# A hand-ordered retention and channel-mix kernel on one core: a different word order, block 5 in one chunk, all scaling on VectorE

## The chip, the cores and the metric

The kernel runs on one core of a Trainium2 chip. A core has TensorE (PE, matrix products; its weight loads are shown apart as PEld), VectorE (DVE), ScalarE (ACT), GpSimd (POOL) and SyncE (SP). Each works through its own list of instructions in order and waits on semaphores for the others. The metric is device microseconds (us) of one execution; lower is better.

## The reference

Retention with a decaying state per head, then a token-shifted channel mix:

```python
for t in range(S):                      # B, H, S, D = 4, 8, 768, 64
    state = gamma * state + outer(k[t], v[t])
    y[t] = scale * q[t] @ state
x = y as (B, S, 512)
xk = mu_k * x + (1 - mu_k) * x_prev     # x_prev: x one token earlier
xr = mu_r * x + (1 - mu_r) * x_prev
k = relu(xk @ w_k)                      # 512 -> 1024
v = (k * k) @ w_v                       # 1024 -> 512
out = sigmoid(xr @ w_r) * v             # w_r: 512 -> 512
```

## The kernel before

The 4 x 768 tokens are cut into 12 blocks of 256 tokens, three to a batch entry; the state is carried from block to block inside an entry. The whole program is one list of words, ORDER. A loop at the end of the kernel reads it from left to right and lets each word issue the instructions of one step, so ORDER sets the order on every engine and on the two queues that issue loads and stores (GpSimd and SyncE). No scheduler moves anything; the framework only adds the semaphore waits that data and buffers need.

A word is a code with numbers, then the PSUM banks after @, or the engine after ~ (v VectorE, a ScalarE, p GpSimd, s SyncE). `K.0.3@7` is key group 3 of block 0 into bank 7. The codes, with block n first:

| code | function (line of its instructions) | what it does | engine |
|---|---|---|---|
| lq, lk, lv | load (L232, L237) | q, k, v of a block from DRAM; two DMAs where it is split, one else. EARLY halves go through k2s and are cast by cq, ck | GpSimd or SyncE queue |
| wk, wr, wv | load_wk, load_wr, load_wv | the weights, w_k and w_v in halves | GpSimd queue |
| vs | scale_v (L255) | v times powers of gamma | VectorE or GpSimd |
| Tq, Tk, Eq, Ek | trans, turned_q, turned_k (L274, L280, L243) | transpose q, k and copy out of PSUM | PE, ScalarE |
| S, M | scores (L320, L333, L341), masked (L349, L356) | scores and their mask | PE, VectorE |
| C, U, G | state (L368, L386, L397), summed (L421, L245), decayed (L426) | the chunk's part of the state, its sum, its decay to the next block | PE, VectorE or ScalarE |
| I, Y, J | inter_off, intra, inter_on (L443, L464, L480, L491) | the output from the state and from the scores | PE |
| D, dx | yout (L509, L516), differ (L531) | x from PSUM, its difference to the token before | VectorE |
| X.n.w.j | mixed (L560) | quarter j of the mixed input, w 0 for keys, 1 for the gate | VectorE |
| K, Qa, Qb | keys (L574, L584), relued (L593), squared (L601, L605) | products with w_k, relu, square | PE, ScalarE |
| R, s | gate (L614), opened (L620) | products with w_r, sigmoid | PE, ScalarE |
| V, O, st | values (L626), result (L632), store (L639) | half the products with w_v, times the gate, store of 128 tokens | PE, VectorE, SyncE queue |
| Vc, Oc, sc | values_c (L644), result_c (L651), store_c (L659) | the same for a cut of the last tokens' columns | PE, VectorE, a queue |
| gy, mu, mt, me | powers (L708, L718, L711), load_mu, trans_mu, copy_mu | constants | |
| z.c | zeros (L693, L700) | products with zeros; c // 4 of them in f32, c % 4 in f16, written to a bank and read by nobody | PE |

A block is worked in one of three ways. HALF cuts it into chunks of 64 tokens (one M, up to four U, two D instructions), WIDE into chunks of 128 (two M, two U where a block of its entry follows, one D), and blocks 0 and 1 in a third way, with 128 columns but 64 rows. GROUPS pairs blocks whose X and K are issued once for both. Q16, K16, V32 are rings of four buffers, VS, QT, KT of three, DX of two, XM of three; k2s holds three blocks of squared keys.

Of the kernel before, what the change touches and what calls it, by code (L numbers as in the profile page):

```python
# [53 lines left out]
Qa.6.1 Qb.6.1 K.6.2@6 Qa.6.2 lq.10~p O.3.1 U.8.1 st.1.0 X.5.1.0 X.5.1.2 lk.10~p U.8.2 I.8@01 O.3.0  # L54
st.2.1 Tq.9@23 Eq.9~a O.4.1 Qb.6.3 S.8@45 M.8~v K.6.0@7 K.6.6@6 Qa.6.0 Qb.6.0 Qa.6.6 X.6.1.3
S.9@23 st.3.1 Tq.11@45 Y.8 Eq.11~a X.6.1.2 R.5.1@7 s.5.1 K.6.7@6 Qb.6.2 K.6.4@4 Qa.6.4 M.9~v D.8~v
dx.8~v X.8.0.0 X.8.0.3 X.8.0.1 X.8.1.1 V.5.0.0@5 R.5.0@7 K.6.5@4 s.5.0 X.6.1.1 Tk.10@01 Qa.6.7
lv.10~p vs.10~v X.6.1.0 C.9@23 U.9.0~v Ek.10~a st.3.0 Tq.10@67 V.5.0.1 O.5.0 X.8.0.2 V.5.1.0@0
R.6.1@1 Qa.6.5 U.9.1 U.9.2 U.9.3 Eq.10~a V.5.1.1 st.5.0 O.5.1 s.6.1 Qb.6.4 S.10@45 I.9@67 C.10@23
G.9~a vs.11~v U.10.0 U.10.1 U.10.2 Qb.6.5 M.10~v st.5.1 R.6.0@1 s.6.0 R.7.0@0 s.7.0 K.8.1@1 Qa.8.1  # L60
K.8.2@2 Qa.8.2 C.11@01 I.10@45 U.10.3 Y.9 K.8.0@3 D.9~v Qb.6.7 K.8.3@2 st.4.1 Tk.11@67 G.10~a
U.11.0 U.11.1 Qa.8.0 Ek.11~a U.11.2 Y.10 D.10~v R.7.1@3 s.7.1 dx.9~v dx.10~v X.9.1.1 I.11@01
X.8.1.0 S.11@67 M.11~v X.9.0.0 Qb.8.2 V.7.0.0@4 Qa.8.3 X.9.0.2 X.9.0.1 V.7.1.0@5 V.6.0.0@3 X.9.0.3
Qb.8.1 Qb.6.6 V.6.1.0@2 V.7.1.1 X.8.1.2 V.7.0.1 V.6.0.1 V.6.1.1 K.9.5@6 K.9.7@7 Qb.8.0 st.4.0
# [725 lines left out]
```

## Time and profile before

| | us |
|---|---|
| runs of the kernel before | 155.8, 156.06, 156.61 (median 156.06) |
| profiled execution, own time | 156.68 |
| its span, first to last instruction | 154.9 |
| granted TensorE clock, mean | 1.00 |

| stretch, us | PE busy | VectorE busy | ScalarE busy | GpSimd busy | moved, GB/s |
|---|---|---|---|---|---|
| 5 to 10 | 3.83 of 5 | 3.00 | 3.28 | 4.85 | 250 |
| 20 to 25 | 4.87 of 5 | 4.83 | 4.92 | 3.61 | 213 |
| 70 to 80 | 9.91 of 10 | 9.76 | 7.52 | 6.83 | 142 |
| 100 to 110 | 9.97 of 10 | 9.11 | 7.97 | 0 | 109 |
| 145 to 150 | 5.00 of 5 | 2.25 | 1.68 | 0 | 232 |

A matmul's row shows it from its start to a modelled end, so PE can show as busy while its next operand is awaited; distances from start to start tell more. GpSimd's busy time is the issuing of its DMAs (about 0.9 us each) and two scalings. Loads on the GpSimd queue land in the order of their issue; the median from issue to landing is 7 to 8 us for q, k and v. In the profile's names, ps is PSUM, a the masked scores, tg and t the state, xT the retention output, kr the relued keys, rs the opened gate, os the result.

### The profile page before, as it was taken

The page shows a single profiled execution, that of the slowest core. Times are in us where ns is not written, and L with a number is a line of the kernel's source. Part 1 is how long each engine was busy: PE and PEld are TensorE (multiplying, and loading weights), DVE is VectorE, ACT ScalarE, POOL GpSimd, SP SyncE. Part 2 cuts the span into 40 slices and gives each one's busy share as a digit, 9 for nine tenths or more (in the row PEclk, how much of TensorE's full clock was granted, in tenths as well). Part 3 has the DMA queues.
Part 4 walks back from the last instruction along what each step waited for, and adds up shares of the span by engine and source line. Part 5 has one row for each costly group of instructions (what it writes and reads, how often), then busy time and mean ns, then how long its engine had stood idle before and what let it go on. Part 6 is the DMA issues. An engine that isn't in the chain of part 4 may idle for free.

```text
span 154.9 us, 5520 instructions
## 1 busy us (share of the span) xinstructions
PE 146.0 (94%) x2423; PEld 83.9 (54%) x2423; DVE 126.9 (82%) x205; ACT 99.4 (64%) x186; POOL 55.5 (36%) x65
## 2 busy tenths in 40 slices
...
GB/s 144 263 219 194 197 228 171 196 241 218 156 180 212 199 241 258 223 234 181 116 147 204 150 68 4 4 74 203 4 4 0 6 82 136 52 0 72 96 209 169
DMA packets 45768, 22.31 MB, mean 144 GB/s; under 512 B 37416, under 2 KB 41392, under 8 KB 45744
## 3 DMA queue, kind: packets, MB, share of 16 engines
...
## 4 chain that ended last, share of the span: by engine, by line
PE 55%; DVE 24%; DMA 12%; issue 4%; POOL 3%; DVEq 0%; POOLq 0%
PE ps L626 19%; DMA v<-in_v_dram 12%; PE ps L614 9%; PE ps L574 9%; PE ps L584 8%; DVE a L356 3%; DVE xk L560 3%; DVE xr L560 3%; DVE vs L255 3%; DVE dx L531 2%; DVE xT L516 2%; DVE tg L421 2%; DVE os L632 2%; PE ps L443 2%; DVE a L349 1%
## 5 line engine op out<-in xcount | busy, mean ns | idle before, releaser
L626 PE MATMUL ps<-wv,k2s 128*128 128x512 f16 x184 | 43.4, 379 | 0.0
L593 ACT ACTIVATE kr<-ps 128x512 f32<-128x512 f32 x48 | 27.8, 596 | 23.1 <-PE ps L574 18.0
L626 PEld LDWEIGHTS <-k2s 128*128 128x128 f16 x184 | 17.4, 98 | 20.0
L632 DVE SCALAR_TENSOR_TENSOR os<-ps,rs 128x512 f32<-128x512 f32 x23 | 15.4, 683 | 14.5 <-ACT rs L620 7.4
L614 PE MATMUL ps<-wr,xr 128*128 128x512 f16 x96 | 24.1, 380 | 0.0
L584 PE MATMUL ps<-xk,wk 128*128 128x256 f16 x192 | 24.0, 273 | 0.0
L232 POOL DMA_DIRECT2D k<-in_k_dram x20 | 17.7, 898 | 15.2 <-PE ps L280 10.5
L574 PE MATMUL ps<-xk,wk 128*128 128x512 f16 x96 | 22.5, 379 | 0.0
L584 PEld LDWEIGHTS <-wk 128*128 128x128 f16 x192 | 18.1, 98 | 4.9 <-DMA wk<-in_moe_w_k_dram 0.6
L620 ACT ACTIVATE rs<-ps 128x512 f32<-128x512 f32 x24 | 13.7, 594 | 9.3 <-PE ps L614 8.9
L560 DVE SCALAR_TENSOR_TENSOR xr<-dx,mu,xT 128x256 f16<-128x256 f32 (+1 forms) x36 | 19.2, 564 | 0.1
L560 DVE SCALAR_TENSOR_TENSOR xk<-dx,mu,xT 128x256 f16<-128x256 f32 (+1 forms) x36 | 18.8, 567 | 0.2
L232 POOL DMA_DIRECT2D v<-in_v_dram x18 | 16.2, 915 | 1.4 <-DMA q<-in_q_dram 0.5
L243 ACT COPY kT<-ps 128x1024 f16<-128x1024 f16 (+1 forms) x13 | 12.2, 947 | 5.2 <-PE ps L280 4.1
L601 ACT ACTIVATE k2s<-kr 128x512 f16<-128x512 f32 x24 | 14.9, 628 | 0.3
L574 PEld LDWEIGHTS <-wk 128*128 128x128 f16 x96 | 9.2, 98 | 10.8
L531 DVE TENSOR_TENSOR dx<-xT 128x1024 f32<-128x1024 f32 x12 | 14.6, 1223 | 0.3
L605 ACT ACTIVATE k2s<-kr 128x512 f16<-128x512 f32 x24 | 14.5, 628 | 0.1
L243 ACT COPY qT<-ps 128x1024 f16<-128x1024 f16 (+1 forms) x13 | 12.3, 949 | 2.4 <-PE ps L274 2.2
L614 PEld LDWEIGHTS <-xr 128*128 128x128 f16 x96 | 8.8, 97 | 9.2 <-DVE xr L560 0.2
L255 DVE TENSOR_TENSOR vs<-v,csm_sb 128x1024 f16<-128x1024 f32 x10 | 12.1, 1216 | 2.0 <-DMA v<-in_v_dram 2.0
L356 DVE TENSOR_TENSOR a<-ps,c_sb 128x1024 f16<-128x1024 f32 (+1 forms) x12 | 12.2, 1040 | 0.5 <-PE ps L333 0.4
...
## 6 DMA issues: line engine op xcount, KB each, us to landing
...
wk<-in_moe_w_k_dram POOLq DMA_DIRECT2D x2, 512.0 KB, 11.0
...
```

The source lines that it names most:

```text
L232: e.dma_start(out=dst[:, :, i * D : i * D + D], in_=src[:, i * P : i * P + P].rearrange("h p d -> p h d"),)
L243: e.copy(out=out, in_=in_)
L255: e.tensor_tensor(out=VS(n), in0=V32(n).rearrange("p h (i d) -> p i h d", i=2), in1=gks[:, int(half(n) or wide(n)), :, :, None].to_broadca ...
L356: nc.vector.tensor_tensor(out=a_full(n)[:, i, :, j0:j1], in0=pairs(banks("S", n, i, j0))[:, :, j0:j1], in1=(below if wide(n) else causal[: ...
L531: e.tensor_tensor(out=DX(k)[:, :, m * TM + t0 : m * TM + t1], in0=x[:, :, c + t0 : c + t1], in1=x[:, :, c - 1 + t0 : c - 1 + t1], op=ALU.s ...
L560: nc.vector.scalar_tensor_tensor(out=XM[w](k)[:, j, t0:t1], in0=DX(k)[:, j, t0:t1], scalar=mu[:, w * NCO + j : w * NCO + j + 1], in1=x[:, ...
L574: nc.tensor.matmul(banks("K", n, g), lhsT=wk16[:, co, g * P : g * P + P], rhs=XM[0](k)[:, co, :], start=(co == 0), stop=(co == NCO - 1),)
L584: nc.tensor.matmul(pz[:, i, :], lhsT=wk16[:, co, fo * P : fo * P + P], rhs=XM[0](k)[:, co, m * TM + t0 : m * TM + t1], start=(i == 0 and c ...
L593: nc.scalar.activation(out=kr, in_=banks("K", n, g, *u), func=AF.Relu)
L614: nc.tensor.matmul(banks("R", n, tb), lhsT=XM[1](k)[:, co, t : t + P], rhs=wr16[:, co, :], start=(co == 0), stop=(co == NCO - 1),)
L626: nc.tensor.matmul(banks("V", n, tb), lhsT=K2(n)[:, fo, tb * P : tb * P + P], rhs=wv16[:, fo, :], start=(fo == 0), stop=(fo == NFO - 1),)
L632: nc.vector.scalar_tensor_tensor(out=OS(2 * n + tb), in0=banks("V", n, tb), scalar=1.0 / (KSC * KSC), in1=RS(2 * n + tb), op0=ALU.mult, op ...
```

## The change

The five edits: block 5 goes from HALF to WIDE; the last 128 tokens' columns are cut into 256, 128 and 128 (CUTS) and stored by SyncE, SyncE and ScalarE, instead of 256 and 256; every vs is on VectorE (vs.1 and vs.3 were on GpSimd); gy.1 and G.10 move from ScalarE to VectorE, U.0.0, U.3.0 and U.9.0 from VectorE to ScalarE; and the whole of ORDER is new. The first K word of block 0 stands behind the scores, masks, state and output words of block 1, where it stood between them. The loads change their order too: half of block 0's k ahead of its v, block 1's q and block 2's q ahead of block 1's k and v. The zero products go from 22 units in seven words to 38 in eleven (z.12 becomes four z.3; z.9, z.4 and z.7 come before K.0.0). The number of DMAs for loads is the same; there is one store more. Shown up to the first K of the pair 6 and 7 and from the first K of block 11:

```diff
-HALF = (5, 6, 7, 8, 9, 10, 11)
+HALF = (6, 7, 8, 9, 10, 11)
...
-WIDE = (2, 3, 4)
+WIDE = (2, 3, 4, 5)
 HEADS = ((0, 1), (3, 2), (4, 5), (7, 6))
+CUTS = ((0, 256), (256, 384), (384, 512))
 ORDER = """
-lq.0.0.2~s gy.0 lv.0~p lk.0.0.2~s ck.0.0.2~v mu lk.0.2.4~p lq.0.2.4~p gy.1~a lv.1~p lk.1~p lq.1~p
-cq.0.0.2~v lq.2~p wk.0~p z.12@6 Tk.0.0.2@0 Tq.0.0.2@1 Ek.0.0.2~a Eq.0.0.2~a mt@2 wk.1~p vs.0~v
-z.2@6 S.0.0.0.2@01 me M.0.0.0.2~v S.0.1.0.2@45 Tk.0.2.4@2 M.0.1.0.2~v Tq.0.2.4@3 lk.2~p C.0@67
-U.0.0~v Ek.0.2.4~a Eq.0.2.4~a z.1@0 S.0.0.2.4@23 M.0.0.2.4~v I.0@45 S.0.1.2.4@01 M.0.1.2.4~v z.1@2
-Y.0 U.0.1 G.0~a vs.1~p Tk.1@7 Ek.1~a D.0~v dx.0~v lv.2~p lq.3~p lk.3~p C.1@01 U.1.0 X.0.0.0
-X.0.0.3 Tq.1@6 Eq.1~a z.4@2 S.1.1@67 lq.4~p X.0.0.2 I.1@45 Tq.2@0 M.1.1~v S.1.0@23 Eq.2~a wr~p
-X.0.0.1 z.1@7 K.0.0@6 M.1.0~v U.1.1 G.1~a lk.4~p Qa.0.0 X.0.1.0 X.0.1.1 Qb.0.0 Y.1 D.1~v dx.1~v
-X.1.0.1 z.1@3 K.0.3@7 X.1.0.2 Qa.0.3 K.0.2@1 X.1.0.0 Qa.0.2 X.1.0.3 Tk.2@6 K.0.1@0 Ek.2~a vs.2~v
-S.2.0@67 S.2.1@45 M.2.0~v Qb.0.3 K.1.1@1 K.1.2@2 Qa.0.1 Qb.0.2 lv.3~p C.2@0 Qa.1.2 Tq.3@3 Eq.3~a
-U.2.0 I.2@67 Tk.3@0 Qa.1.1 K.1.0@2 Tq.4@1 X.1.1.0 Ek.3~a Qa.1.0 M.2.1~v Y.2 lq.5~p Eq.4~a S.3.0@45
-J.2 X.1.1.1 Qb.1.0 Qb.1.2 X.1.1.2 X.1.1.3 S.3.1@23 lv.4~p K.1.3@0 Qa.1.3 Qb.1.3 wv.0~p X.0.1.3
-X.0.1.2 R.0.0@1 D.2~v dx.2~v X.2.0.2 Qb.0.1 s.0.0 X.2.0.0 lq.6~p R.0.1@6 s.0.1 Tk.4@0 X.2.0.3
-R.1.1@7 X.2.0.1 vs.3~p M.3.0~v Ek.4~a K.2.3@1 Qa.2.3 K.2.0@6 Qa.2.0 M.3.1~v S.4.1@45 M.4.1~v
-Tq.5@1 Eq.5~a C.3@23 U.3.0~v U.3.1 s.1.1 vs.4~v R.1.0@6 s.1.0 G.3~a K.2.1@0 I.3@45 Qb.2.3 S.4.0@23
-M.4.0~v Y.3 C.4@67 U.4.0 U.4.1 G.4~a K.2.2@1 Qb.1.1 I.4@23 J.3 Qa.2.1 Qa.2.2 Y.4 Qb.2.0 D.3~v
-V.0.0.0@6 Tq.6@45 J.4 dx.3~v V.1.1.0@7 D.4~v dx.4~v X.3.0.1 V.0.1.0@0 V.1.0.0@1 X.2.1.2 Qb.2.2
-wv.1~p V.0.0.1 Eq.6~a V.0.1.1 lq.7~p lk.6~p Tk.6@45 Ek.6~a O.0.0 Tq.7@23 Eq.7~a V.1.0.1 S.6@45
-lk.5~p Tk.5@6 X.3.0.2 X.3.0.3 X.3.0.0 K.3.3@2 Qb.2.1 K.3.2@3 O.1.0 Ek.5~a O.0.1 X.3.1.1 M.6~v
-lv.5~p vs.5~v K.3.5@0 Qa.3.5 Qa.3.3 K.3.4@6 V.1.1.1 Qa.3.2 lv.6~p C.5@01 S.5@45 Qa.3.4 vs.6~v
-C.6@23 Qb.3.3 Qb.3.2 O.1.1 M.5~v U.5.0 X.2.1.3 U.5.1 U.6.0~a U.6.1 U.6.2 U.5.2 U.6.3 K.3.0@6
-X.2.1.1 Qa.3.0 Qb.3.0 V.2.0.0@7 K.3.6@4 Qa.3.6 K.3.7@6 st.0.1 Qa.3.7 Qb.3.7 I.5@01 I.6@45 V.2.0.1
-K.3.1@3 Qa.3.1 Qb.3.1 X.2.1.0 R.2.0@6 lk.8~p Tk.8@23 lv.7~p Y.5 X.3.1.0 vs.7~v X.3.1.3 Y.6 X.3.1.2
-s.2.0 R.3.1@6 D.5~v dx.5~v st.1.1 st.0.0 Ek.8~a X.5.0.3 O.2.0 X.5.0.0 V.2.1.0@2 X.5.0.1 R.3.0@3
-D.6~v G.6~a Qb.3.4 s.3.0 s.3.1 lv.8~p R.2.1@0 s.2.1 X.5.1.3 X.5.0.2 R.4.0@1 s.4.0 V.2.1.1 lk.7~p
-C.7@67 O.2.1 lk.9~p Tk.9@01 Ek.9~a lv.11~s Tk.7@45 Ek.7~a lq.8~p U.7.0 U.7.1 U.7.2 st.2.0 vs.8~v
-K.5.1@3 dx.6~v Qa.5.1 K.5.2@2 I.7@45 S.7@01 U.7.3 K.5.0@6 M.7~v lv.9~p Qb.3.6 Qa.5.0 K.5.3@3
-Qa.5.2 Qb.5.0 R.4.1@6 lk.11~p Qb.3.5 vs.9~v V.4.1.0@7 X.5.1.1 C.8@01 Y.7 D.7~v dx.7~v X.6.0.3
-X.6.0.0 lq.11~p Qa.5.3 Qb.5.2 Tq.8@23 X.6.0.2 V.4.1.1 s.4.1 V.4.0.0@6 Eq.8~a V.3.1.0@2 Qb.5.3
-Qb.5.1 V.4.0.1 X.6.0.1 lq.9~p G.7~a V.3.0.0@3 V.3.1.1 V.3.0.1 U.8.0 K.6.3@4 Qa.6.3 O.4.0 K.6.1@5
...
-R.9.1@0 Qa.9.1 Qb.9.1 X.11.1.2 V.8.0.1 K.11.1@5 O.7.0 Qa.11.1 R.8.0@4 V.8.1.1 Qb.9.3 s.8.0
-R.10.0@5 K.11.0@1 st.6.0 Qa.9.0 Qb.9.0 st.7.1 K.11.2@2 st.7.0 R.9.0@4 Qa.11.0 Qb.9.6 Qb.11.0
-Qb.11.1 X.11.1.1 O.8.0 K.11.3@1 s.9.1 V.9.1.0@3 V.10.1.0@0 s.8.1 O.8.1 st.8.1 R.11.1@6 V.9.0.0@7
-Qa.11.3 V.11.0.0@1 s.10.0 Qa.11.2 Qb.11.2 R.10.1@2 V.9.1.1 O.9.1 V.10.1.1 s.10.1 O.10.1 st.9.1
-Qb.11.3 V.9.0.1 st.10.1 s.11.1 Vc.11.1.1@2 s.9.0 V.10.0.0@6 O.9.0 R.11.0@0 V.11.0.1 st.8.0 st.9.0
-s.11.0 Oc.11.1.1 sc.11.1.1~a O.11.0 st.11.0 V.10.0.1 O.10.0 st.10.0 Vc.11.1.0@0 Oc.11.1.0
-sc.11.1.0~s
+lq.0.0.2~s gy.0 gy.1~v lk.0.2.4~p z.3@6 z.3@6 z.3@6 z.3@6 Tk.0.2.4@0 lk.0.0.2~s ck.0.0.2~v
+Tk.0.0.2@1 lv.0~p mu mt@2 me cq.0.0.2~v vs.0~v Ek.0.0.2~a Tq.0.0.2@3 Eq.0.0.2~a z.3@6 S.0.0.0.2@23
+S.0.1.0.2@45 M.0.1.0.2~v M.0.0.0.2~v Ek.0.2.4~a lq.0.2.4~p Tq.0.2.4@1 Eq.0.2.4~a C.0@67
+S.0.0.2.4@01 M.0.0.2.4~v U.0.0~a I.0@45 S.0.1.2.4@23 M.0.1.2.4~v z.1@0 Y.0 lq.1~p U.0.1 lq.2~p
+Tq.2@7 D.0~v dx.0~v Tq.1@6 X.0.1.1 lk.1~p lv.1~p Tk.1@2 Ek.1~a X.0.0.1 Eq.1~a z.9@0 S.1.0@23
+vs.1~v M.1.0~v z.1@6 C.1@45 wk.0~p G.0~a U.1.0 z.4@6 I.1@23 X.0.0.3 U.1.1 G.1~a X.0.1.3 Eq.2~a
+S.1.1@01 M.1.1~v z.7@6 Y.1 X.0.0.2 X.0.0.0 K.0.0@7 Qa.0.0 Qb.0.0 lv.2~p vs.2~v K.0.1@6 lk.2~p
+wk.1~p D.1~v Qa.0.1 C.2@0 U.2.0 dx.1~v X.1.0.1 Tk.2@7 I.2@01 z.1@4 K.0.3@6 Ek.2~a S.2.0@23
+S.2.1@45 X.1.0.3 lq.3~p Qa.0.3 lk.4~p Qb.0.3 K.0.2@7 Qa.0.2 Qb.0.2 X.1.0.2 X.1.0.0 K.1.0@6 K.1.1@7
+M.2.0~v Qa.1.0 Tq.3@2 X.1.1.3 M.2.1~v Qb.0.1 Qa.1.1 Qb.1.1 lq.4~p Tq.4@6 Eq.4~a Y.2 X.0.1.0 Tk.4@3
+Ek.4~a Eq.3~a J.2 X.0.1.2 X.1.1.1 X.1.1.2 D.2~v dx.2~v X.2.0.2 K.1.3@7 X.2.0.0 wr~p K.1.2@4 Qa.1.2
+lk.3~p X.2.0.3 Qb.1.0 R.0.1@6 S.4.0@01 X.2.0.1 Tk.3@5 Ek.3~a R.0.0@4 s.0.0 lv.3~p s.0.1 M.4.0~v
+vs.3~v K.2.3@2 X.1.1.0 Qa.2.3 K.2.1@3 Qa.1.3 Qa.2.1 S.3.1@45 lq.5~p M.3.1~v S.3.0@01 M.3.0~v
+C.3@67 U.3.0~a Qb.1.2 U.3.1 Tq.5@2 Eq.5~a R.1.0@3 s.1.0 R.1.1@6 s.1.1 G.3~a I.3@45 S.4.1@01
+K.2.0@7 Qa.2.0 lv.4~p Qb.2.3 vs.4~v lk.5~p C.4@23 M.4.1~v U.4.0 Y.3 Qb.2.0 Tk.5@6 Ek.5~a I.4@01
+J.3 wv.0~p Y.4 X.2.1.1 K.2.2@2 Qa.2.2 U.4.1 G.4~a S.5.0@67 D.3~v dx.3~v Qb.1.3 lq.6~p Tq.6@45
+Eq.6~a J.4 D.4~v V.1.0.0@3 dx.4~v M.5.0~v V.0.1.0@2 Qb.2.1 X.3.0.0 V.1.1.0@0 wv.1~p V.1.0.1
+V.0.0.0@1 V.1.1.1 O.1.0 lk.6~p Qb.2.2 X.3.0.1 Tk.6@67 Ek.6~a lk.7~p Tk.7@45 Ek.7~a V.0.0.1 V.0.1.1
+X.3.0.2 X.3.0.3 O.0.0 K.3.6@3 Qa.3.6 K.3.3@6 S.5.1@45 O.1.1 Qa.3.3 lv.5~p vs.5~v O.0.1 lq.7~p
+M.5.1~v C.5@3 U.5.0 X.2.1.2 Tq.7@01 Eq.7~a K.3.5@7 Qa.3.5 lv.6~p vs.6~v K.3.4@6 Qa.3.4 Qb.3.4
+X.2.1.0 st.1.1 X.2.1.3 K.3.2@2 I.5@01 S.6@67 M.6~v Qa.3.2 S.7@45 Qb.3.5 Y.5 K.3.1@3 C.6@67 M.7~v
+Qb.3.2 U.6.0~a lv.7~p J.5 D.5~v Qa.3.1 K.3.0@2 Qa.3.0 Qb.3.6 V.2.0.0@4 V.2.1.0@5 R.2.1@2 U.6.1
+vs.7~v V.2.1.1 s.2.1 Qb.3.0 U.6.2 U.6.3 G.6~a I.6@01 st.0.1 lq.8~p dx.5~v C.7@23 Tq.8@67 Eq.8~a
+V.2.0.1 O.2.1 K.3.7@5 Qa.3.7 X.5.0.3 Qb.3.1 Qb.3.7 R.2.0@6 s.2.0 X.5.0.2 X.5.0.1 X.5.0.0 K.5.2@7
+Qa.5.2 Qb.3.3 U.7.0 U.7.1 U.7.2 X.3.1.3 X.5.1.1 K.5.1@5 K.5.0@2 U.7.3 lv.9~p st.0.0 K.5.3@6
+X.3.1.2 lk.8~p Qa.5.0 G.7~a X.3.1.1 Qa.5.1 X.3.1.0 O.2.0 st.2.0 I.7@23 Y.6 D.6~v Qb.5.1 dx.6~v
+V.4.1.0@7 R.3.0@4 Tk.8@01 Ek.8~a s.3.0 Y.7 R.4.1@5 lv.8~p vs.8~v V.4.1.1 s.4.1 Qb.5.0 R.4.0@0
+D.7~v st.2.1 O.4.1 Qa.5.3 Qb.5.3 vs.9~v lk.9~p dx.7~v X.6.0.2 X.6.0.3 X.6.0.0 X.6.1.1 st.1.0
+Qb.5.2 s.4.0 V.4.0.0@4 lv.10~p R.3.1@5 Tk.9@23 C.8@67 s.3.1 C.9@01 U.9.0~a V.4.0.1 Ek.9~a X.6.0.1
+U.8.0 O.4.0 st.4.0 U.9.1 V.3.1.0@5 V.3.0.0@2 V.3.1.1 V.3.0.1 K.6.6@3 K.6.1@4 Qa.6.1 Qa.6.6 Qb.6.6
...
+X.11.0.2 X.11.0.0 K.11.2@2 s.9.0 K.11.1@3 V.8.1.1 Qa.9.0 Qb.9.0 Qb.9.2 V.10.1.0@7 R.11.0@1 Qb.9.6
+Qa.11.1 Qa.11.2 st.6.1 R.8.0@3 V.9.1.0@2 O.8.1 V.9.0.0@4 Qa.9.4 Qb.9.4 K.11.3@6 st.8.1 Qa.11.3
+Qb.11.3 R.10.1@0 s.8.0 V.9.0.1 Qb.11.1 V.10.0.0@6 Qb.11.2 K.11.0@3 Qa.11.0 O.8.0 R.9.1@5 O.9.0
+st.9.0 s.11.0 Qb.11.0 st.8.0 V.10.1.1 V.9.1.1 s.9.1 O.9.1 st.9.1 Vc.11.1.1@1 R.11.1@3 s.11.1
+Oc.11.1.1 s.10.1 V.11.0.0@5 O.10.1 st.10.1 R.10.0@2 s.10.0 V.11.0.1 O.11.0 sc.11.1.1~s st.11.0
+V.10.0.1 O.10.0 st.10.0 Vc.11.1.0@4 Oc.11.1.0 sc.11.1.0~s Vc.11.1.2@7 Oc.11.1.2 sc.11.1.2~a
 """
...
     def values_c(e, n, tb, c):
-        x = slice(c * dm // 2, (c + 1) * dm // 2)
+        x = slice(*CUTS[c])
...
     def result_c(e, n, tb, c):
-        x = slice(c * dm // 2, (c + 1) * dm // 2)
+        x = slice(*CUTS[c])
...
     def store_c(e, n, tb, c):
-        x = slice(c * dm // 2, (c + 1) * dm // 2)
+        x = slice(*CUTS[c])
...
```

More of the change, by code (lines that the diff above doesn't have):

```diff
@@ L53 @@
-Qb.5.1 V.4.0.1 X.6.0.1 lq.9~p G.7~a V.3.0.0@3 V.3.1.1 V.3.0.1 U.8.0 K.6.3@4 Qa.6.3 O.4.0 K.6.1@5
[L54 to L64, printed above, removed]
```

17 lines of the change are left out of this document (14 added, 3 removed).

## The prediction

> **What bounds the kernel now.** I read the page's busy table first, then the chain of waits, then busy time by stretch, then the timeline at five milestones.
>
> ```profile
> PE 146.0 (94%) x2423; PEld 83.9 (54%) x2423; DVE 126.9 (82%) x205; ACT 99.4 (64%) x186; POOL 55.5 (36%) x65
> ...
> PE 55%; DVE 24%; DMA 12%; issue 4%; POOL 3%; DVEq 0%; POOLq 0%
> ```
>
> TensorE (PE) is busy 94% of 154.9 us, but the chain runs over it for only 55%: the rest of its busy time is matmuls waiting in its pipe or zero products. By stretch (PE, PEld, DVE, ACT, POOL):
>
> ```profile
> 15.00:20.00 5.00, 3.80 (x87) 2.51 (x89) 5.00 (x10) 1.55 (x2) 2.33 (x3) 1.00 1.49 193
> ...
> 50.00:60.00 10.00, 9.87 (x233) 5.23 (x232) 10.00 (x14) 7.09 (x12) 7.44 (x9) 1.00 1.30 234
> ...
> 130.00:140.00 10.00, 10.00 (x64) 6.06 (x63) 2.42 (x5) 9.03 (x18) 0.00 (x0) 1.00 0.07 26
> ```
>
> VectorE (DVE) is full from 15 us on and hands over only at 130, so until there PE can run no faster than VectorE delivers mixed inputs; the granted clock is 1.00 throughout. The milestones are the first K (key product) of a block, because by then the same products are left in both orders:
>
> ```profile
> 8.16 1.23 DVE L255 TENSOR_TENSOR vs<-v,csm_sb 128x1024 f16<-128x1024 f32 x1 [2.00 <-DMA v<-in_v_dram]
> ...
> 18.42 1.10 PE L584 MATMUL ps<-xk,wk 128*128 128x256 f16 x8
> ...
> 24.79 1.95 PE L584 MATMUL ps<-xk,wk 128*128 128x256 f16 x16
> ...
> 52.85 3.63 PE L574 MATMUL ps<-xk,wk 128*128 128x512 f16 x16
> ...
> 131.21 1.04 PE L584 MATMUL ps<-xk,wk 128*128 128x256 f16 x8
> ```
>
> These are VectorE's start (v of block 0 landed at 8.14) and K.0, K.1, K.3 and K.11; K.6 begins at 86.50 in the chain. The last Vc product ends at 151.3. A group of K or R, or half a V, takes 0.864 us in a full stretch (four matmuls of 216 ns start to start). Sums of such pitches put 94.0 us of products after K.3, where 98.4 us passed: **4.4 us were lost there**, 2.3 before K.6 and 2.1 behind it.
>
> **The change, part by part.** VectorE start to start, from stretches where it never waits: vs and M 1.13 (0.60 for M of half the heads), dx and whole D 1.14, D of a 64-token block 1.22, X 0.40 (0.66 for a pair), U 0.33, O 0.60.
>
> GpSimd's two scalings go to VectorE:
>
> ```profile
> L255 DVE TENSOR_TENSOR vs<-v,csm_sb 128x1024 f16<-128x1024 f32 x10 | 12.1, 1216 | 2.0 <-DMA v<-in_v_dram 2.0
> ...
> L255 POOL TENSOR_TENSOR vs<-v,csm_sb 128x1024 f16<-128x1024 f32 x2 | 3.8, 1918 | 3.7 <-DMA v<-in_v_dram 3.6
> ```
>
> Each ends 0.70 us sooner but takes 1.13 of the full engine: +2.3 us. The Trainium skill (GPSIMD Engine Reference, Engine selection) gives elementwise work to VectorE, GpSimd being about twice as slow; the rows agree on the operation (1918 against 1216 ns), and by that rule alone the edit would gain 2 x 0.7 = 1.4 us. Here the engine that receives it has no free time, so I take the cost. GpSimd had the second one on the chain (1.91 at 36.97, behind the load that landed at 36.83); now vs.3 is due at 37.9.
>
> Block 5 as one 128-token chunk: a second M (+1.13), two U less (-0.67), D -0.08; on PE about +0.6 from wider S, I and Y. gy.1 moves from ScalarE to VectorE (+0.65, by the 512-wide row; before 8 us, hidden behind the wait for v), G.10 too (+0.33); U.0.0, U.3.0, U.9.0 go to ScalarE (-1.0; there 0.39 each, hidden in its 23 us of waits ahead of L593). VectorE from vs.0 to the last X.11.0 then holds 116.2 us of pitches against 112.4.
>
> Zero products: 38 units instead of 22. The first 12 run while data arrive; the other 26 stand where PE waits for VectorE in my walk, so nothing. Uncovered, the 16 more would cost 16 x 0.216 = 3.5 us.
>
> The end: the last block's columns in three cuts. The new 128-wide matmul is in no row; bounds are 0.055 (half of L644's 0.109) and 0.098 (a weight load), so eight and eight of them cost 0.87 to 1.57 against 0.87. I take +0.3. The last VectorE step and store shrink: 0.42 to about 0.29 (estimate on the 512- and 256-wide rows), the store about 0.1 (2.0 for 256 KB, 1.8 for 128). Net about 0.
>
> **The new order** is the large term. I walk VectorE's and PE's lists with these pitches, taking each wait where the operand comes later. The loads keep their queue pace (before: 0.9 us between k halves, 1.15 v halves, 1.43 q, 2.5 a weight half). v of block 0 now stands behind half of k: 8.45. v of block 1 lands at 15.2 instead of 10.85, needed at 16.4; the second w_k half at 24.4 instead of 20.26, needed at 25.5; v of block 5 at 54.1, needed at 55.8. So hidden, by 1.1 us or more; a queue 2 us slower costs 1.
>
> To K.0.0, VectorE's list is vs.0, four M halves, U.0.1, D.0, dx.0, two X.0.1, vs.1, M.1.0, U.1.0, X, U.1.1, X, M.1.1, two X: 12.6 us of pitches, 13.2 at about 1.05, 0.8 waiting for Y.0. That ends at 22.4: **K.0 at 22.4, not 18.4**. Block 1's two M, its scaling and its U stand ahead. PE has nothing dense until then.
>
> Then vs.2, D.1, U.2.0, dx.1, four X.1.0 (5.5 us): K.1 at 27.95 against 24.8. D.3 starts at 45.4 (before 43.95). From J.4 (47.5) PE has eight halves of V in stock, 6.9 us, plus 0.6 of transposes: K.3 at 55.0, and X.3.0 is ready at 54.6. Lag 2.15 against 52.85. Owed work is equal: V.1.1.1 is done (-0.86), block 5 and the cuts are still due (+0.9). Next, K.3, Y.5, V.2, R.2 fill PE to K.5 at 70.9 and V.4, V.3 to K.6 at 86.9, losing 0.7. K.11 comes at 130.2 by PE and 129.3 by VectorE, losing 0.3.
>
> So the walk loses 1.0 us after K.3, where the kernel before lost 4.4. It knows no handovers: before, VectorE ran K.3 to K.6 at 1.04 of its pitches, where my walk has 1.00, +1.2. Behind K.6 I take 1.5, between the walk's 0.3 and the 2.1 of before. Loss 0.7 + 1.2 + 1.5 = 3.4; PE's end 55.0 + 94.1 + 3.4 = 152.5 against 151.3: **+1.2 us**. The profiled execution, 156.68 (span 154.9 and 1.8 around it), becomes 157.9; it lies 0.6 above the median of 156.06, so against the runs 157.3.
>
> **Rivals.**
>
> *The waits after K.3 vanish (faster).* One mechanism: by K.3 the new order has put V.0 and V.1 in stock, so PE never again waits for VectorE, as in the walk. Loss 1.0: PE's end 150.1, -1.2 us, 154.9. It decides from a loss below 2.2; beyond 0.5% from 1.4. For it: VectorE owes no more behind K.6 than before (45.1 against 46.6). Against: 41 of its 43 us from 86 to 129 were busy before, so a late M or D has no slack.
>
> *VectorE paces it to the end.* Before, 112.4 us of pitches took 8.16 to 129.2, a factor 1.077. At that factor 116.2 end at 133.5, K.11 starts there, 20.4 us of products follow: 153.9, +2.6; with the 2.0 us that lay between X.11 and K.11 before, +4.3. Between them 159.4. It decides from X.11.0 later than 132.1. For it: VectorE is full in nearly every stretch; against: PE's stock of V at the end.
>
> *Instruction waits or late loads show early.* The chain holds 4.5% of "issue", 7.0 us; a third more is 2.3 on top of 1.2, 159.6. Before 55 us PE has no stock to hide it. The single waits named "issue" ahead of weight loads are at most 0.8 us, and the instruction queue moved 19 blocks of 16 KB, which argues against. The Trainium skill (Runtime: NRT & Kernel Launch, Instruction fetch mechanics) holds that crossing a block is mostly hidden; by it this rival falls. The rows lean that way without being clean: the block of 14.03 to 14.99 is followed by two such waits (0.76 and 0.50), that of 20.39 to 21.37 by none over 0.25.
>
> **How the numbers follow.** Forecast 0.40 (157.3; its own range 156.4 to 158.4), first rival 0.30, second 0.22, third 0.08. A difference of 0.5%, 0.8 us, is about what measuring this kernel can tell: faster is under 155.3, slower over 156.8. Faster: 0.25 of the first rival. Same: its other 0.05 and 0.12 of the forecast, 0.17. Slower: 0.28 + 0.22 + 0.08 = 0.58. The range reaches to the first rival's own time and past the second's: 154.8 to 159.8.
>
> **What would show it.** K.0 at 22 to 23 and K.1 at 28; vs.1 starting at about 16.4 without waiting for its load; K.3 at 54.5 to 56; K.6 at 87 to 88.5; X.11.0 done at 130 to 132; PE's last product near 152.5; no tensor operation on GpSimd; vs 12 times on VectorE at about 1216 ns. I am wrong if K.0 comes before 20.5, if the lag at K.3 is below 1 or above 4, or if from K.3 to the end the new order loses as little as the walk.

## The result and the profile after

| | before | after |
|---|---|---|
| median of 7 runs, us | 156.51 (155.80 to 159.22) | 157.36 (156.95 to 157.62) |
| ratio of the times, 95% interval | | 1.0057 [1.0029, 1.0084] |
| profiled execution, own time; its span | 156.68; 154.9 | 156.95; 155.2 |
| PE's last product ends | 151.29 | 151.68 |

The changed kernel is 0.6% slower: 0.85 us by the medians, 0.27 by the two profiled executions. The one shown of before lies 0.2 above its median and the one shown of after is the fastest of its seven, so the milestones below show less of the loss than the runs do. One run of before, 159.22, is slow beside its others and left out of the ratio.

From the page of the changed kernel, busy time by engine, the chain by engine, and the group of all scalings:

```profile
PE 148.4 (96%) x2383; PEld 85.1 (55%) x2383; DVE 129.0 (83%) x205; ACT 98.0 (63%) x181; POOL 51.7 (33%) x63
...
PE 88%; DVE 8%; ACT 1%; issue 1%; DVEq 0%
...
L256 DVE TENSOR_TENSOR vs<-v,csm_sb 128x1024 f16<-128x1024 f32 x12 | 14.6, 1219 | 1.1 <-DMA v<-in_v_dram 1.1
```

The change did what it says: VectorE has all 12 scalings and works 2.1 us more, GpSimd 3.8 less. The chain moved from a mixture (PE 55%, VectorE 24%, DMA 12%) to PE, 88%. DMA (12%) and GpSimd (3%) are gone from it, unnamed waits fell from 4% to 1%, and still the kernel is not faster. Busy time by stretch, with the same columns as before (PE, PEld, DVE, ACT, POOL, granted clock, DMA share, GB/s):

```profile
15.00:20.00 5.00, 4.63 (x81) 2.11 (x80) 4.96 (x10) 2.58 (x9) 2.61 (x3) 1.00 1.55 217
50.00:60.00 10.00, 10.00 (x181) 4.93 (x183) 10.00 (x15) 5.70 (x8) 5.11 (x7) 1.00 1.20 233
130.00:140.00 10.00, 10.00 (x60) 5.65 (x58) 1.83 (x4) 6.07 (x12) 0.00 (x0) 1.00 0.22 80
```

VectorE is full in the first two stretches, as before, and hands over at the same place. From 15 to 20 PE is now busy too, but in good part with zero products. The milestones, and two places between K.6 and K.8, from the timeline of the changed kernel (start, duration, what; in brackets the idle time before it and what ended it):

```profile
7.89 1.23 DVE L256 TENSOR_TENSOR vs<-v,csm_sb 128x1024 f16<-128x1024 f32 x1 [1.08 <-DMA v<-in_v_dram]
...
15.99 1.22 DVE L256 TENSOR_TENSOR vs<-v,csm_sb 128x1024 f16<-128x1024 f32 x1
...
21.86 1.91 PE L585 MATMUL ps<-xk,wk 128*128 128x256 f16 x16
...
54.22 1.89 PE L575 MATMUL ps<-xk,wk 128*128 128x512 f16 x8
...
87.02 1.89 PE L575 MATMUL ps<-xk,wk 128*128 128x512 f16 x8
...
89.14 3.61 PE L575 MATMUL ps<-xk,wk 128*128 128x512 f16 x16 [0.23 <-DVE os L633]
...
100.22 0.23 PE L321 MATMUL ps<-qT,kT 64*64 64x64 f16 x7
100.64 0.40 PE L321 MATMUL ps<-qT,kT 64*64 64x64 f16 x25 [0.19 <-issue]
...
131.58 1.91 PE L585 MATMUL ps<-xk,wk 128*128 128x256 f16 x16
```

K.0 comes 3.4 us later than before, K.3 1.4, K.6 0.7, K.11 and the end 0.4. So a late start was mostly made up, and twice in the middle PE stands for about 0.4 us: K.6.7 waits for a PSUM bank that O.3.1 still reads, and in the middle of the 32 products of S.10 it waits for nothing that the profile names (e12 comes back to that).

### The profile page after: what moved, and what is told of

The parts are those of the page before. It is cut to its first block, busy times and chain, and to the rows that moved or that the text cites. A ratio compares the mean times of both kernels' runs of the same rounds, so it can differ in the third digit from the quotient of the medians.

```text
span 155.2 us, 5436 instructions
## 1 busy us (share of the span) xinstructions
PE 148.4 (96%) x2383; PEld 85.1 (55%) x2383; DVE 129.0 (83%) x205; ACT 98.0 (63%) x181; POOL 51.7 (33%) x63
## 4 chain that ended last, share of the span: by engine, by line
PE 88%; DVE 8%; ACT 1%; issue 1%; DVEq 0%
PE ps L627 24%; PE ps L585 14%; PE ps L615 14%; PE ps L575 13%; PE ps L701 4%; PE ps L444 3%; PE ps L275 3%; PE ps L281 3%; DVE xk L561 2%; PE ps L334 2%; PE ps L694 1%; PE ps L481 1%; PE ps L321 1%; PE ps L369 1%; PE ps L465 1%
## 5 line engine op out<-in xcount | busy, mean ns | idle before, releaser
L627 PE MATMUL ps<-wv,k2s 128*128 128x512 f16 x184 | 44.1, 380 | 0.0
L585 PE MATMUL ps<-xk,wk 128*128 128x256 f16 x192 | 23.5, 273 | 0.1
L575 PE MATMUL ps<-xk,wk 128*128 128x512 f16 x96 | 23.0, 379 | 0.2 <-DVE os L633 0.2
L256 DVE TENSOR_TENSOR vs<-v,csm_sb 128x1024 f16<-128x1024 f32 x12 | 14.6, 1219 | 1.1 <-DMA v<-in_v_dram 1.1
L357 DVE TENSOR_TENSOR a<-ps,c_sb 128x1024 f16<-128x1024 f32 (+1 forms) x14 | 14.7, 1066 | 0.1
L606 ACT ACTIVATE k2s<-kr 128x512 f16<-128x512 f32 x24 | 14.5, 627 | 0.3
L602 ACT ACTIVATE k2s<-kr 128x512 f16<-128x512 f32 x24 | 14.3, 624 | 0.2
```

The source lines that it names most:

```text
L256: e.tensor_tensor(out=VS(n), in0=V32(n).rearrange("p h (i d) -> p i h d", i=2), in1=gks[:, int(half(n) or wide(n)), :, :, None].to_broadca ...
L357: nc.vector.tensor_tensor(out=a_full(n)[:, i, :, j0:j1], in0=pairs(banks("S", n, i, j0))[:, :, j0:j1], in1=(below if wide(n) else causal[: ...
L575: nc.tensor.matmul(banks("K", n, g), lhsT=wk16[:, co, g * P : g * P + P], rhs=XM[0](k)[:, co, :], start=(co == 0), stop=(co == NCO - 1),)
L585: nc.tensor.matmul(pz[:, i, :], lhsT=wk16[:, co, fo * P : fo * P + P], rhs=XM[0](k)[:, co, m * TM + t0 : m * TM + t1], start=(i == 0 and c ...
L627: nc.tensor.matmul(banks("V", n, tb), lhsT=K2(n)[:, fo, tb * P : tb * P + P], rhs=wv16[:, fo, :], start=(fo == 0), stop=(fo == NFO - 1),)
```

## The experiments

Each kernel is the changed kernel with one edit, but for one that edits the kernel before. Columns: the first K of a block, and the end of PE's last product, in us of the profiled execution; then the runs.

| kernel | K.0 | K.1 | K.3 | K.6 | K.8 | K.11 | end | median us | ratio to before |
|---|---|---|---|---|---|---|---|---|---|
| before | 18.42 | 24.79 | 52.85 | 86.34 | 105.47 | 131.21 | 151.29 | 156.51 | |
| after | 21.86 | 27.47 | 54.22 | 87.02 | 102.11 | 131.58 | 151.68 | 157.36 | 1.0057 [1.0029, 1.0084] |
| e1, two cuts | 21.90 | 27.52 | 54.26 | 86.87 | 101.91 | 131.39 | 151.47 | 157.37 | 1.0059 [1.0036, 1.0083] |
| e2, scaling on GpSimd | 22.22 | 27.85 | 56.16 | 88.86 | 103.57 | 133.05 | 153.15 | 158.94 | 1.0156 [1.0131, 1.0181] |
| e3, block 5 in 64s | 21.91 | 27.52 | 54.26 | 90.51 | 106.41 | 135.88 | 155.99 | 162.13 | 1.0328 [1.0261, 1.0396] |
| e4, fewer zeros | 23.87 | 31.11 | 57.88 | 90.52 | 105.22 | 134.70 | 154.80 | 160.06 | 1.0211 [1.0173, 1.0249] |
| e5, keys first | 18.11 | 32.45 | 59.19 | 92.00 | 106.91 | 136.39 | 156.49 | 161.14 | 1.0298 [1.0261, 1.0334] |
| e6, extra before K.3 | 21.72 | 27.34 | 58.70 | 91.32 | 105.89 | 135.39 | 155.49 | 161.55 | 1.0327 [1.0284, 1.0370] |
| e7, extra before K.6 | 21.91 | 27.53 | 54.27 | 91.40 | 105.72 | 135.22 | 155.32 | 159.52 | 1.0198 [1.0160, 1.0236] |
| e8, extra before K.11 | 21.91 | 27.52 | 54.27 | 86.88 | 101.99 | 135.87 | 155.97 | 160.59 | 1.0269 [1.0213, 1.0326] |
| e9, keys first again | 18.68 | 27.86 | 54.61 | 87.42 | 102.47 | 131.95 | 152.05 | 157.83 | 1.0093 [1.0052, 1.0133] |
| e10, before, scaling on VectorE | 18.87 | 25.23 | 53.65 | 86.93 | 106.01 | 131.75 | 151.83 | 157.24 | 1.0061 [1.0036, 1.0085] |
| e11, bank free | 21.28 | 26.90 | 53.64 | 86.36 | 100.67 | 130.16 | 150.26 | 156.94 | 1.0030 [0.9996, 1.0065] |
| e12, instructions shifted | 24.48 | 30.09 | 56.84 | 89.63 | 105.87 | 135.34 | 155.44 | 160.79 | none |

The kernel before had medians of 156.43 to 156.47 beside these runs.

### e1: two cuts at the end

```diff
-CUTS = ((0, 256), (256, 384), (384, 512))
+CUTS = ((0, 256), (256, 512))
-... sc.11.1.1~s ... sc.11.1.0~s Vc.11.1.2@7 Oc.11.1.2 sc.11.1.2~a
+... sc.11.1.1~a ... sc.11.1.0~s
```

> The changed kernel with the end of the kernel before: two cuts of 256 columns, the last store on SyncE. In the two profiles the last product ends 0.4 us later with three cuts (151.7 against 151.3) and the last VectorE step 0.25 us later (152.0 against 151.75). If the third cut is the cost: 157.1, that is 0.25 us below the changed kernel's 157.36, and a ratio to the kernel before of 1.004. If the smaller last store pays for it (the purpose that a narrow cut can have): 157.4 to 157.6. Everything ahead of 145 us stays as in the changed kernel.

157.37 against 157.36: no gain of 0.25, and just below the second expectation. From K.11 to the end it is 20.08 us here and 20.10 with three cuts: products 128 columns wide follow each other after 55.9 ns, just half of a 256-wide one, so the third cut costs PE nothing and buys nothing.

### e2: the two scalings on GpSimd again

```diff
-vs.1~v ... vs.3~v
+vs.1~p ... vs.3~p
```

The loads that stood behind them on GpSimd's queue are issued ahead of them, so that none waits behind a scaling. Block 1's v landed 1.2 us later for that (15.68), but its scaling still began at 15.76, ahead of the changed kernel's 15.99.

> The changed kernel with vs.1 and vs.3 on GpSimd; the loads that stood behind them in GpSimd's queue (wk.0, blocks 2's k and v, wk.1, q of 3; later q of 5, v of 4, k of 5, wv.0, q of 6) are issued ahead of them so that the queue does not wait for the scaling. Takes 2 x 1.13 = 2.3 us off VectorE ahead of K.3. If VectorE paces the stretch up to K.3: K.3 1 to 2 us earlier than 54.3 and the time 156.0 to 156.8. If PE's stock of V halves sets K.3 by then (X.3.0 was ready at 53.9, PE free at 54.3): K.3 within 0.5 us of 54.3 and the time 157.0 to 157.4. If taking GpSimd's scaling away was a gain, because it ends 0.70 us sooner on VectorE: 157.6 to 158.5.

158.94, above all three expectations: giving the work back to GpSimd costs 1.58 us, though VectorE has 2 x 1.13 less to do. The timeline of this kernel shows what happened; L560, L255 and L584 are here the mixed inputs, the scaling and K:

```profile
34.63 3.36 DVE L560 SCALAR_TENSOR_TENSOR xk<-dx,mu,xT 128x256 f16<-128x256 f32 x4
...
35.38 1.92 POOL L255 TENSOR_TENSOR vs<-v,csm_sb 128x1024 f16<-128x1024 f32 x1
...
38.04 1.14 PE L584 MATMUL ps<-xk,wk 128*128 128x256 f16 x9 [1.45 <-DVE xk L560]
```

and the same four X.2.0 in the changed kernel:

```profile
34.25 1.67 DVE L561 SCALAR_TENSOR_TENSOR xk<-dx,mu,xT 128x256 f16<-128x256 f32 x4
```

Seen one by one, all of the delay lies on the third of the four, the one that begins 0.04 us after the scaling; a single X takes 0.48 us else:

```profile
35.42 2.17 DVE L560 SCALAR_TENSOR_TENSOR xk<-dx,mu,xT 128x256 f16<-128x256 f32 x1
```

It ends at 37.59, 0.29 us after the scaling (35.38 to 37.30). So VectorE's four operations need 3.36 us instead of 1.67, and PE waits 1.45 us for them. K.3 comes 1.9 later; the other scaling, of block 1, makes K.0 0.4 later. The masks that lay beside the same scaling in the kernel before kept their time (three in 3.69 us, 1.23 each). What differs is what VectorE reads: X reads two arrays (dx and xT), both in SBUF; a mask reads one of its two from PSUM. The Trainium skill (SBUF — State Buffer, "SBUF: two separate sides") says the same: one port pair is shared by the two engines as an exclusive lock, and a VectorE operation with two SBUF inputs and a GpSimd operation that reads SBUF shut each other out for the whole instruction. The rows agree: one X stands still until the scaling is over, 1.69 us longer than its 0.48, beside a scaling of 1.92. That the mask escapes because of its PSUM input rests on these two cases alone.

### e10: the kernel before with both scalings on VectorE

```diff
-vs.1~p ... X.2.0.1 vs.3~p M.3.0~v ... Qa.2.0 M.3.1~v
+vs.1~v ... X.2.0.1 M.3.0~v ... Qa.2.0 vs.3~v M.3.1~v
```

> The kernel before with its two GpSimd scalings on VectorE (vs.1 in its place, vs.3 behind M.3.0), nothing else. The prediction's price (VectorE is full, +1.13 each): K.0 later by 0.6, K.3 by 1.5 to 2, 157.7 to 158.4. Rival (GpSimd held VectorE up, or stood on the chain, so the edit is a gain by itself): K.3 no later than 52.9, 155.5 to 156.6.

157.24, 0.78 slower than the kernel before beside it (156.46), between the two expectations: K.0 0.45 later, K.3 0.80, the end 0.54. (Its profiled execution had half the granted clock from 11.6 to 15.0 us; the other nine, at 0.995 or more on average, took as long.) So the same edit costs 0.8 us in the old order, where GpSimd works beside masks, and saves 1.6 in the new one, where it would work beside X.

### e3: block 5 in 64-token chunks

```diff
-HALF = (6, 7, 8, 9, 10, 11)
-WIDE = (2, 3, 4, 5)
+HALF = (5, 6, 7, 8, 9, 10, 11)
+WIDE = (2, 3, 4)
-S.5.0@67 ... M.5.0~v ... S.5.1@45 ... M.5.1~v C.5@3 U.5.0 ... Y.5 K.3.1@3 ... J.5 D.5~v
+S.5@45 ... M.5~v C.5@23 U.5.0 U.5.1 U.5.2 ... K.3.1@3 ... Y.5 D.5~v
```

> The changed kernel with block 5 in 64-token chunks as before: one M and two D instructions instead of two and one, three U instead of one, and its output product Y.5 in one piece where J.5 stood. VectorE 0.4 us shorter by pitches, PE about 0.6 us shorter. If work of this size counts fully: 156.4 to 156.8. If it falls into the slack between the engines (PE has V halves in stock around it): 157.2 to 157.4.

162.13, far above both expectations. The loss is not block 5's work alone. A piece of the chain of this kernel in order of time (start, duration, what):

```profile
63.44 0.07 PE ps L444 x5
63.51 1.98 issue
65.49 0.28 PE ps L444 x9
```

In the middle of one group of 16 equal short products PE stands for 1.98 us and waits for nothing that the profile shows; at 100.86 it does so for another 1.00. Close to both stands a transfer of the instruction queue: blocks of 16 KB went from 63.02 to 63.99 and from 98.63 to 99.58. The 64-token block adds 128 instructions to PE's list, so every later block of instructions ends at another place of the program. Of the 4.3 us by which the end moved in the profile, 3.0 are the first wait and what the second is longer than the wait of S.10 in the changed kernel (from start to start, 2.16 and 0.81). About 1.3 is left for block 5 and for the other place of Y.5, and it isn't told apart further.

### e12: the instructions shifted alone

```diff
-z.3@6 z.3@6 z.3@6 z.3@6 Tk.0.2.4@0
+z.3@6 z.3@6 zz.67@6 z.3@6 Tk.0.2.4@0
+    def small(e, count):
+        z16 = zero.bitcast(F16)
+        for _ in range(count):
+            nc.tensor.matmul(
+                banks("zz", count)[0:64, 0:64], lhsT=z16[0:64, 0:64], rhs=z16[0:64, 0:64],
+                start=True, stop=True, skip_group_check=True,
+            )
```

> The changed kernel with one of the first zero words (three products) replaced by 67 small products with zeros (64 x 64 by 64 columns, 8.6 ns each at full clock) while PE waits for the first keys: 128 instructions more on PE, as many as block 5 in 64-token chunks adds, and the same order of everything else. So the places where PE's instruction blocks end lie 128 instructions earlier in the program. Theory (with block 5 in 64-token chunks, PE stood still for 1.98 and 1.00 us in the middle of groups of short products because a block of instructions was not there yet): waits named issue of 0.5 us or more show in PE's rows, 2 to 5 us in all, and 159 to 163. Rival (that wait belonged to block 5's own products): no such wait on PE, and 157.2 to 157.6.

The edit did more than was meant: in the profiled execution (160.71) the 67 products took 3.78 us, 54 ns each from start to start and not 8.6, and K.0 came 2.6 us late. Four runs gave 157.31 to 161.26, three of them over 160.7, too unlike for an interval; the fourth took as long as the changed kernel, so this loss isn't in every execution. From K.0 to K.6 the profiled one keeps the changed kernel's pace (65.15 us, 65.16 there). Then, in its timeline:

```profile
3.73 3.78 PE L694 MATMUL ps<-zero 64*64 64x64 f16 x67
...
100.32 0.28 PE L281 MATMUL ps<-c_sb,q 64*64 64x64 f16 x9 [1.34 <-issue]
```

PE stands for 1.34 us with 9 of the 32 products of the same transpose left as in e3, which has the same number of added instructions; K.8 comes 1.15 later than the 2.6 explain. So the second wait of e3 belongs to the place of the instruction and not to block 5. The first one, 1.98, did not come again.

The traces settle more than that. Counted in PE's rows, the waits of e12, of the second place in e3 and of S.10 in the changed kernel, e1, e8 and e9 all stand behind PE's 1758th product, whichever product that is; so does a short one in e5. The rows of e9 have six zero products fewer ahead of it, and its wait stands six products later in S.10, with 19 of the 32 left instead of 25. Lines of e3 and e9:

```profile
100.86 0.28 PE L281 MATMUL ps<-c_sb,q 64*64 64x64 f16 x9 [1.00 <-issue]
...
101.07 0.35 PE L318 MATMUL ps<-qT,kT 64*64 64x64 f16 x19 [0.17 <-issue]
```

In all seven PE goes on 1.24 to 1.45 us after the last 16 KB of the instruction queue ahead of it have landed (1.28 in e3, 1.34 in e12, 1.31 in the changed kernel). In e2, e4, e6, e7 and e11 PE comes to that product by itself 1.34 to 2.07 us after the landing, and there is no wait. The first wait of e3 stands 640 products earlier, 1280 instructions with their weight loads, and ends 1.50 us after its landing; that is five blocks, if a block holds about 255 instructions (estimate: the kernel before has 4846 products and weight loads and moved 19 blocks). So PE waits there for a block of instructions, and whether the wait shows depends on when PE arrives. Why the queue moved the block no earlier isn't shown.

### e4: fewer zero products

The 26 units behind the first 12 are left out (z.3, z.1, z.9, z.1, z.4, z.7, z.1).

> The changed kernel without the 26 units of zero products behind the first 12. If they only fill PE's waiting time: the time of the changed kernel, 157.2 to 157.5, with K.0 at 21.9 as before. If some of them stand in the way (z.9 ahead of S.1.0, z.7 ahead of Y.1, 1.5 to 2 us each): K.0 0.3 to 0.8 us earlier and 156.8 to 157.2. If the array needs them to stay at full clock: the granted clock below 1.00 between 10 and 25 us, K.0 or K.1 later by 0.5 to 2 us, 157.8 to 159.3.

160.06: the third expectation's cause, at a price above its range. No product of the reference is touched, and K.0 is 2.0 later, K.1 3.6. The windows of this kernel, the granted clock in the third column from the right:

```profile
10.00:12.00 2.00, 0.91 (x20) 0.68 (x20) 1.77 (x4) 0.38 (x2) 1.84 (x3) 0.55 1.80 200
12.00:20.00 8.00, 5.05 (x132) 4.62 (x131) 5.99 (x8) 2.88 (x6) 3.67 (x5) 0.50 1.40 236
20.00:26.00 6.00, 4.20 (x75) 3.27 (x76) 5.66 (x10) 2.16 (x6) 4.16 (x6) 0.50 1.78 182
26.00:28.00 2.00, 2.00 (x31) 1.34 (x29) 0.21 (x1) 1.55 (x3) 1.76 (x3) 0.68 1.53 197
```

Without the zeros PE ran at half clock from 10.2 to 27.3 us, where the changed kernel has 1.00 throughout. VectorE itself has less busy time from 12 to 20 (5.99 of 8; 7.41 in the changed kernel), because scores, sums and outputs come from PE late. The lag is 3.7 at K.3 and 3.1 at the end. How many of the 26 units the clock needs wasn't tried; the kernel before keeps it at 1.00 with 10 behind its first 12.

### e5 and e9: the first keys ahead of block 1

Both put X.0.0, K.0.0 and K.0.1 ahead of most of block 1. In e5 C.1 stood behind K.0 and zeros behind a relu; e9 mends that:

```diff
-Eq.1~a z.9@0 S.1.0@23 vs.1~v M.1.0~v z.1@6 C.1@45 wk.0~p G.0~a U.1.0 z.4@6 I.1@23 X.0.0.3 U.1.1 G.1~a X.0.1.3 Eq.2~a
-S.1.1@01 M.1.1~v z.7@6 Y.1 X.0.0.2 X.0.0.0 K.0.0@7 Qa.0.0 Qb.0.0 lv.2~p vs.2~v K.0.1@6
+Eq.1~a z.9@0 Eq.2~a X.0.0.3 X.0.0.2 X.0.0.0 S.1.0@23 vs.1~v M.1.0~v z.4@6 C.1@45 K.0.0@7 K.0.1@6 G.0~a U.1.0 I.1@23
+U.1.1 G.1~a Qa.0.0 X.0.1.3 S.1.1@01 M.1.1~v Qb.0.0 Qa.0.1 Y.1 lv.2~p vs.2~v
```

with wk.0 issued behind lv.1.

> The changed kernel with block 0's mixed inputs for keys (X.0.0) and K.0.0, K.0.1 ahead of block 1's scaling, masks and state, as the kernel before had them; some zero products go. K.0 starts at about 17.5 instead of 21.9. If the late start of dense products is what the change pays with: PE gains the two key groups, K.3 is 1 to 1.75 us earlier and the time 155.6 to 156.4. If VectorE paces the stretch (its list is as long as before, only in another order): K.0 is 4 us earlier, but K.1 stays near 27.5 and K.3 near 54.3, and the time is 157.0 to 157.5.

> The first keys again, without the flaws of the run before: the keys' four X.0.0 ahead of block 1's scaling, K.0.0 and K.0.1 behind C.1, their relu behind G.1, no zeros that wait for a relu. Theory (VectorE sets the pace until K.11, PE's early hole costs nothing by itself): VectorE has the same list, so K.0 comes at about 18.7 and K.3 still at 54.2 to 54.9; 157.2 to 158.0 against 157.4. Rival (the late dense start is what the new order pays): K.3 by 53.2 or sooner and 156.0 to 156.6. If the granted clock falls between 18 and 27, the run is the price of PE's holes again and not of the order.

e5 (161.14) answers nothing: C.1 stood behind K.0, whose weights landed only at 18.06, the zeros waited 2.10 us for the relu, and PE then ran at half clock; K.1 came at 32.45. e9 is the clean one, its granted clock 1.00: K.0 at 18.68, 3.2 us sooner than in the changed kernel and 0.3 behind the kernel before; K.3 at 54.61, 0.4 *later*, and 157.83 (157.36; four of its six runs have a mean clock of 1.00 and took 157.25 to 158.00). The time that PE gains by the early keys it waits for at block 1, as a line of e9's timeline shows:

```profile
22.39 0.64 PE L489 MATMUL ps<-a,vs 64*64 64x128 f16 x32 [1.33 <-DVE a L354]
```

So the late K.0, the most visible thing in the new profile, costs nothing by itself: an early one does not bring K.3 sooner. VectorE's list, which is as long in both, sets K.3.

### e6, e7, e8: ten small operations more on VectorE

```diff
+dd.10    (ten 128x128 products of two constants on VectorE, read by nobody)
```

placed ahead of U.4.0 (e6), behind dx.6 (e7), ahead of dx.9 (e8).

> The changed kernel with ten extra VectorE operations (128x128, about 0.2 us each by the row of gy_sb, some 2.1 us in all, results unused) behind M.4.1, ahead of K.3. It measures what a microsecond of VectorE is worth there. If VectorE paces the whole kernel up to 130 us: +1.7 to +2.1, 159.1 to 159.5. If PE's stock of V halves covers it (X.3.0 is ready 0.4 us before PE is free): K.3 later by 1.5 or so but the end later by less, 157.4 to 158.6.

> The same ten operations behind dx.6, ahead of K.6, where VectorE handed over at 86.8 and PE was free at 87.0. If VectorE paces it: +1.7 to +2.1, 159.1 to 159.5. If products in stock (the rest of V.3 and V.4 are done by then, so there is little) cover it: 157.4 to 158.2.

> The same ten operations behind Y.10, ahead of dx.9 and K.11. X.11.0 was ready at 131.1 and PE free for K.11 at 131.6, so 0.5 us are covered: +1.2 to +1.6, 158.6 to 159.0, if K.11 and the mixed inputs of 9 and 11 wait for VectorE; nothing, 157.4, if the V halves of 6 to 8 fill the wait, which is the rival.

The ten took 3.2 us and not 2.1. The next milestone moved by 4.3 to 4.5 us in all three profiles and the end by 3.8, 3.6 and 4.3; 0.5 and 0.8 of it came back between K.6 and K.8, where the changed kernel has PE's two waits. The medians moved by 4.2, 2.2 and 3.2, in e6 and e8 beyond both expectations (e7's profiled run is the slowest of its six). A part of this is not VectorE's work but PE's clock. In e6:

```profile
43.23 3.22 DVE L737 TENSOR_TENSOR mu<-gy_sb 128x128 f32<-128x128 f32 x10
...
46.84 0.42 PE L444 MATMUL ps<-qT,tg 64*64 64x128 f16 x12 [3.10 <-DVE tg L422]
```

PE idled for 3.10 us, and from 48.2 us on its granted clock was half for 3.41 us. The same came about in the profiled executions of e7, from 85.7, and e8, from 123.6, as their pages show (the granted clock in 40 slices of about 4 us, in tenths, 9 for full; e6, e7, e8):

```profile
PEclk9999999999995999999999999999999999999999
...
PEclk9999999999999999999997799999999999999998
...
PEclk9999999999999999999999999999999599999999
```

The runs without it tell what VectorE's work costs by itself. Five of e7's six have a mean clock of 1.00 and took 159.13 to 159.62; three of e8's have it and took 159.71 to 159.96, the other three, at 0.989, over 161.2. By the medians of these, 3.2 us more on VectorE cost 2.1 ahead of K.6 and 2.4 ahead of K.11. So about 1 us is covered at both places, and the rest counts to the end. All runs of e6 have 0.989 or less, so what is covered ahead of K.3 can't be read from them.

### e11: a free bank for K.6.7

```diff
-lq.9~p X.5.1.3 O.3.1 K.6.7@5
+lq.9~p O.3.1 X.5.1.3 K.6.7@5
```

> The changed kernel with O.3.1 one place earlier, ahead of X.5.1.3, so that K.6.7 finds its bank free. Theory (VectorE sets the pace to K.11): PE's 0.4 us at 88.9 are got back and lost again ahead of K.8 or K.9, K.11 at 131.5 to 131.7 and 157.2 to 157.5. Rival (each wait of PE counts to the end): K.11 0.4 earlier, 156.9 to 157.1.

156.94, against 157.36. The intervals of the two ratios overlap, so the gain of 0.4 is likely and not certain; its runs spread over 155.51 to 158.60. The profiled run is the fastest of its ten, with its first loads 0.2 to 0.3 sooner, so only distances are compared. From its timeline:

```profile
86.36 5.34 PE L575 MATMUL ps<-xk,wk 128*128 128x512 f16 x24
...
99.16 0.43 PE L321 MATMUL ps<-qT,kT 64*64 64x64 f16 x32
```

The keys run through without the wait, the gap in S.10 is gone as well, and K.6 to K.8 takes 14.31 us instead of 15.09; from there on nothing is lost again. By this profile that is the rival's answer: a wait of PE counts to the end, too. Since 2.4 of 3.2 us more on VectorE count behind K.6 as well (e8), neither engine has more than about 1 us of slack there; each one's list waits for the other's in turn. This is the best version of the new order that was run; the kernel before (156.46 beside it) remains the fastest.

## Why the prediction came out

The time forecast was 157.3 and 157.36 came; the reasons held in part, and the closeness is luck, as the fifth point shows.

- **K.0 at 22.4:** 21.86. The order of VectorE's list was right; v of block 0 landed at 7.87, where 8.45 was taken, and that is the difference. K.1 came at 27.47 for 27.95, for the same reason.
- **vs.1 at about 16.4 without waiting:** 15.99, no wait; its v landed at 14.52. No load held anything up but the first v.
- **K.3 at 55.0, a lag of 2.15:** 54.22 and 1.37. This is the term that was mis-sized, by 0.8: 0.55 of it is the early v; the rest isn't told apart.
- **A loss of 3.4 behind K.3:** 151.68 - 54.22 - 94.1 = 3.4. The split was right too: to K.6 32.80 us passed where the walk has 31.2 of products, so 1.6 lost (forecast 1.9), and 1.8 behind (forecast 1.5), 0.8 of these the two waits of PE between K.6 and K.8. Taking over the handovers of the kernel before, and not the clean walk, is what made this term.
- **PE's end at 152.5:** 151.68, the mis-sized lag. The end moved by 0.4 where 1.2 was forecast. For the profiled execution 157.9 was forecast and 156.95 came; to get from there to the runs 0.6 was taken off, by the kernel before, where 0.4 had to be added. The two errors cancel, so that 157.3 met 157.36 is luck. What the working got right is that the new order is no gain, and where it loses.
- **The first rival** (waits vanish) needed a loss below 2.2 and got 3.4. **The second** needed X.11.0 later than 132.1; it was done at 131.13. (Its upper figure should be +4.6 and not +4.3: 2.0 on top of 2.6.) Its premise, little slack on VectorE, is borne out by e7 and e8, about 1 us; but VectorE's list became denser (116.2 us of pitches from 7.89 to 131.13, a factor 1.06, where 1.077 was taken over), so it did not decide. **The third** (instruction waits early) did not happen: between 5 and 55 us one wait named issue of 0.5 us or more is left in PE's two rows, 0.76 ahead of a weight load at 11.58, where the kernel before had five (0.97, 0.52, 0.76, 0.50, 0.63; the first, at 7.55, is more than the 0.8 that the prediction names as the most).
- **The instruction rule of the Trainium skill** (Runtime: NRT & Kernel Launch, Instruction fetch mechanics), that crossing a block is mostly hidden, holds for the changed kernel up to the 0.4 us in S.10. It does not hold for every order: 1.98, 1.00 and 1.34 us in e3 and e12, where PE comes among short products to a block that has just landed.
- **Two scalings on VectorE, +2.3 us:** the step that failed. Taken back they cost 1.58 (e2), and in the old order the edit costs 0.78 (e10). The price was read from the full engine alone; what the same work on GpSimd does to VectorE's operations beside it was not asked. The forecast did not suffer, since it walks VectorE's list as it stands; only the share of this edit in the result was wrong. The Trainium skill's rule (GPSIMD Engine Reference, Engine selection), which spoke for VectorE with 1.4 us, gave the right sign in this order, for a reason other than the longer operation.
- **Zero products "so nothing":** whether they delay anyone can't be read from e4, but leaving 26 units out gains nothing: the kernel loses 2.7, as the clock falls to half. That zeros hold the clock was not weighed at all.
- **The end cuts, about 0:** right, with +0.02 on PE, not +0.3. **Block 5 as one chunk** was priced at +0.4 on VectorE and +0.6 on PE; e3 can't confirm it, since moving it back moves the instructions too.

In short: the new order loses 1.0 us less behind K.3 (3.4 instead of 4.4) and reaches K.3 1.4 later; the difference, 0.4 at PE's end, is the loss in the profile.
